# Who copies a finished block out of PSUM, and when two DMAs are issued: two attentions on one core

## The chip, the cores and the metric

The kernel runs on one core of a Trainium2 chip. The metric is the device time of one execution in microseconds. Before the change three runs took 1610.16, 1611.54 and 1611.78 us (median 1611.54).

## The reference

Two attentions over 2048 positions with 576 columns, 32 heads of 18 each, side by side in the output. A is local: each position attends to itself and seven earlier ones at distances of 2, 4, ... 14. B is full softmax attention.

```python
H = 32; Dh = D // H            # D = 576, S = 2048
qkv = (x @ wqkv).reshape(B, S, 3, H, Dh)
# A: idx = pos[:, None] - arange(8) * 2, masked where negative
logits = einsum("bhsd,bhswd->bhsw", q, k[:, :, idx]) * scale
a = einsum("bhsw,bhswd->bhsd", softmax(logits), v[:, :, idx]) @ A_wo
# B: every query with every key
p = softmax(einsum("bhqd,bhkd->bhqk", q, k) * scale)
b = einsum("bhqk,bhkd->bhqd", p, v) @ B_wo
return concatenate([a, b], axis=-1)
```

## The kernel before, in words

All matmuls of projections, scores and output products work on split numbers: a value is held as a rounded high part and a low part (`hi`, `lo`), and a product is the sum of three.

**Stage 1** (the first 410 us or so) makes q, k and v of both attentions and stores them in DRAM (`dqk`, `dv`, `da`).

**Stage 2** is a loop over 512 steps (line 1226). B's 32 heads are 8 groups `g` of four, its queries 4 blocks `b` of 512, its keys 16 tiles `kt` of 128: a step is one `(g, b, kt)`, so a block is 16 steps. In a step

- `score` (L298) makes for each of four heads a product of 128 keys with 512 queries (L305, TensorE) in one of four PSUM banks ("scores"), and ScalarE takes the exponential into `e` (L309);
- three, seldom four, products for later blocks are made in three other banks ("else", L175) and reduced on VectorE to maxima `mx` over keys (L191, L193, L205);
- `weigh` (L769) multiplies the `e` of the step before with v into the bank `po` (L772), which collects a block's 16 steps: for each head 18 sums and the denominator.

The order of the scores and maxima inside a step is written out as a string (L1230 to L1237).

`finish` (L777) follows the last `weigh` of a block: `o` is a copy of `po` in SBUF (L781), and TensorE's next `weigh` needs `po` free. Fixed numbers of steps later (`later`) the denominators go through DRAM (`den`, `drec`, `rec`, L804 to L807), GpSimd multiplies `o` by the reciprocals and splits it (L808 to L810), and it is stored (`do`, L800). Blocks of the last group take a shorter way (`shortly`, `closing`).

The maxima of a block end in the queries' operand `qs`: as rows 54 and 55 they are subtracted inside the score product. `least` (L211) reduces them, `turn` transposes them, `halve` (L225) splits them on GpSimd, `order` (L229) stores them in DRAM (`dm`, L232), and `place` (L235) loads them back into `qs` (L238). Between these stand fixed numbers of steps; from `order` to `place` it is one step in the last group and three elsewhere. A block's first score needs them.

A's local attention is computed in stage 2 by GpSimd, VectorE and ScalarE (`local`, L886) for 8 stretches of 256 positions, 55 steps apart. Its results go to DRAM (`dao`, L980), and `get` (L983) fetches them for 128 positions at a time into the single buffers `at0`, `at1` and `ahl` (L990, L992). Two steps later on, `one` and `two`, hold the output product, one half of the columns each (`sums_of_a`, L1000): 27 matmuls in two banks (L1104), a copy of one sum by ScalarE (L1008), and an add of the other by VectorE (L1009), which is issued behind the step's scores (`behind_scores`, L1251). The steps that hold a product are in the set `producing` (L1040, and L1196 for those of B in the last group); many of them are first steps of a block, in which `finish` runs for the block before.

Every engine works through its instructions in the order in which the program gives them. SP issues nearly all DMAs, and one that has to wait holds all behind it.

Of the kernel before, what the change touches and what calls it, by code (L numbers as in the profile page):

```python
# [10 lines left out]
AF = mybir.ActivationFunctionType  # L11
# [11 lines left out]
NG = H // 4  # L23
# [46 lines left out]
def two_attentions(ctx: ExitStack, tc, xa, wa, woa, xb, wb, wob, out):  # L70
# [5 lines left out]
    nc = tc.nc  # L76
# [29 lines left out]
    po = p_po.tile([128, 512], F32, name="po")  # L106
# [10 lines left out]
    step = 0  # L117

    def later(n, f):
        agenda[step + n].append(f)  # L120
# [44 lines left out]
    def block(g, b):  # L165

        qs, ks = sets[g % 3]
        mx = maxes.tile([128, 2, 2, 4, 6], F32, name="mx", bufs=3)
        left = 2 * 8 * 6
        rest = [[(k, t, p) for k in range(NB) for t in range(4) for p in range(2)] for _ in range(2)]  # L170

        def take(ps, r, k, t, p, at, n):

            rows_ = slice(64 * r, 64 * r + 54)
            return nc.tensor.matmul(ps, qs[rows_, b, p, 128 * t : 128 * t + 128],  # L175
                                    ks[rows_, p, 512 * k + at : 512 * k + at + n], start=True, stop=True)

        def made(n):
            nonlocal left
            left -= n  # L180
            if left == 0:
                later(int(projecting), least)

        def whole(r):
            k, t, p = rest[r].pop(0)
            ps = bank()
            take(ps, r, k, t, p, 0, 512)

            def reduce():
                if k < 2:  # L190
                    nc.vector.tensor_reduce(mx[:, r, p, t, k : k + 1], ps, axis=AX.X, op=ALU.max)  # L191
                else:
                    nc.vector.tensor_reduce(mx[:, r, p, t, 2 * k - 2 : 2 * k], ps.rearrange("q (h n) -> q h n", h=2),  # L193
                                            axis=AX.X, op=ALU.max)
                made(1 + (k > 1))

            return reduce

        def part(i, k, t, p, r, ps, before=None):
            if before:  # L200
                behind_of(nc.tensor.nop(nofuse=True), before)
            ins = take(ps[:, 256 * r : 256 * r + 256], r, k, t, p, 256 * i, 256)

            def reduce():
                nc.vector.tensor_reduce(mx[:, :, p, t, 2 * k - 2 + i], ps.rearrange("q (h n) -> q h n", h=2),  # L205
                                        axis=AX.X, op=ALU.max)
                made(2)

            return ins, reduce

        def least():  # L211
            m = least_rooms[n_least[0] % 2]
            n_least[0] += 1
            nc.vector.tensor_reduce(m[:, :16], mx.rearrange("q r p t k -> q (r p t) k"), axis=AX.X, op=ALU.max,
                                    negate=True)
            later(1, lambda: turn(m))

        def turn(m):

            parts = maxes.tile([128, 2, 32], F32R, name="mt", bufs=2)  # L220
            raw = parts[:, 1].bitcast(F32)
            nc.vector.transpose(raw, m)  # L222
            later(1, lambda: halve(parts, raw))

        def halve(parts, raw):  # L225
            split_on(nc.gpsimd, parts[:, 0], parts[:, 1], raw)
            later(2, lambda: order(parts))

        def order(parts):  # L229

            for k in range(2):
                load(rows(dm[g, b, k, 0, 0], (32, 4), (128, 32), (1, 32)), parts[:, k].bitcast(F32))  # L232
            later(1 if g == NG - 1 else 3, place)

        def place():  # L235
            placed.add((g, b))
            for k in range(2):
                load(qs.bitcast(F32)[54 + k : 128 : 64, b].rearrange("r p n -> r (p n)"),  # L238
                     dm[g, b, k, :16].rearrange("(r i) n -> r (i n)", r=2))

        return rest, whole, part
# [169 lines left out]
    with (tc.tile_pool(name="x", bufs=1, side="right") as xp,  # L411
# [103 lines left out]
        if True:  # L515
# [34 lines left out]
            for c in range(5):  # L550
                one, other = (load, nc.scalar.dma_start) if c % 2 == 0 else (nc.scalar.dma_start, load)
# [159 lines left out]
            for k in range(2, 14):  # L711
                n = 46 if k == 2 else 36 + 4 * k
# [13 lines left out]
            order = [t for i in (0, 8) for j in range(4) for t in (i + j, i + j + 4)]  # L726
# [18 lines left out]
            order = [(c, b) for b0 in range(0, NB, 2) for c in range(2) for b in (b0, b0 + 1)]  # L745
            order += [(c, b) for c in range(2, 14) for b in range(NB)]
            for c, b in order:
                n = min(128, 3 * D - 128 * c)
                work_list.append(((b % 2, ws[c][0], xas[b][0], slice(0, n), every),
                                  lambda ps, n=n: ps[:n], lambda ps, c=c, b=b, n=n: leave_a(c, b, n, ps)))  # L750
# [12 lines left out]
        step = 0  # L763
# [13 lines left out]
    def finish(g, b):  # L777
        o = work.tile([128, 512], F32, name="o", bufs=2)
        if g == NG - 1 and b == NB - 1:
            return closing(b, o, work.tile([128, 512], F32, name="rec", bufs=1))  # L780
        nc.scalar.activation(o, po, AF.Copy)  # L781
        den = work.tile([128, 16], F32, name="den", bufs=2)
        rec = work.tile([128, 512], F32, name="rec", bufs=1)
        parts = []

        def room():
            if g == NG - 1 and b == 0:

                parts[:] = [ap(work.tile([128, 4, 128], F32R, name=f"at{i}", bufs=1), (1, 512)) for i in range(2)]
            else:  # L790
                n = work.tile([128, 2, 512], F32R, name="n", bufs=1)
                parts[:] = n[:, 0], n[:, 1], n
            return parts

        if g == NG - 1 and b > 0:
            return shortly(b, o, rec, *room()[:2])

        def store():
            if g < NG - 1:
                load(do[:, g, :, 512 * b : 512 * b + 512].rearrange("i p n -> p i n"), parts[2].bitcast(F32))  # L800
            else:
                plan(step, full(b, parts))

        for at, f in ((1, lambda: load(den, o[DH:128:32])),  # L804
                      (8, lambda: nc.vector.reciprocal(den, den)),
                      (9, lambda: load(drec[g, b].rearrange("i (p n) -> (i p) n", n=16), den)),
                      (13, lambda: load(rec, rows(drec[g, b], (512, 4), (0, 32), (1, 512)))),  # L807
                      (18, lambda: nc.gpsimd.tensor_mul(o, o, rec)),  # L808
                      (19, lambda: nc.gpsimd.tensor_copy(room()[0], o)),
                      (20, lambda: nc.gpsimd.tensor_sub(parts[1], o, parts[0])),  # L810
                      (26, store)):
            later(at, f)
# [49 lines left out]
    producing = set()  # L862
# [23 lines left out]
    def local(j):  # L886
# [96 lines left out]
        def get(n):  # L983
            st["x"] = []
            st["n"] = n
            last = work.tile([128, 128], F32R, name="ahl", bufs=1)
            for i in range(2):
                t = work.tile([128, 4, 128], F32R, name=f"at{i}", bufs=1)
                for s in range(2):
                    load(t.bitcast(F32)[:, :, SUB * s : SUB * s + SUB],  # L990
                         dao[j, i, 2 * n + s, :512].rearrange("(c p) n -> p c n", p=128))
                load(last.bitcast(F32)[64 * i : 64 * i + 64].rearrange("p (s n) -> p s n", s=2),  # L992
                     rows(dao[j, i, 2 * n, 512], (SUB, 64), (D * SUB, 2), (1, SUB)))
                st["x"].append([t[:, c] for c in range(4)])
            st["x"].append(last)
# [21 lines left out]
        pieces = [(LOWER, lower), (SHARE, share), (UP, upper), (REST, rest), (PUT0, lambda: put(0)), (PUT1, lambda: put(1))]  # L1017
# [12 lines left out]
        start = A_FROM + GAP * j  # L1030
        for n in range(2):
            free, begin = turns[-1] if turns else 0, start + PUT1 + 5
            at = max(free, begin)
            one = next(t for t in TURNS if t >= at + 7)
            two = next(t for t in TURNS if t > one + 1)
            turns.extend((one, two))
            pieces.append((max(at, one - 9) - start, lambda n=n: get(n)))
            for h, t in enumerate((one, two)):
                pieces.append((t - 1 - start, lambda h=h: finished(h)))
                producing.add(t)  # L1040
            pieces.append((two + 5 - start, lambda n=n: load(out[p0 + 128 * n : p0 + 128 * n + 128, :D], ys["a", j, n])))
# [184 lines left out]
    while step < ALL:  # L1226
        n, kt = divmod(step, NT)
        g, b = divmod(n, NB)
        many = min(4 if behind() > 0 else 3, total - int(sum(given)))
        if not inside and many in (1, 3):  # L1230
            order = PLAIN if many > 1 else PLAIN.replace("A", "").replace("B", "")
        else:
            places = positions(many)
            order = "".join("%d%s" % (h, "BA"[h % 2] if h in places else "") for h in range(4))
            if inside:
                at = order.index("3" if 3 in places else "2") if step % NT != AT or AT == 0 else FIRST
                order = order[:at] + "+" + order[at:]  # L1237
# [56 lines left out]
```

## Time and profile before

| | us |
|---|---|
| median of three runs | 1611.54 |
| profiled execution | 1610.11 |
| its span, first to last instruction | 1608.3 |
| TensorE (PE) busy | 1597.4 |
| VectorE (DVE) busy | 1388.4 |
| ScalarE (ACT) busy | 1213.3 |
| GpSimd (POOL) busy | 962.0 |
| exponentials L309, 2048 of 608 ns | 1047.2 |
| maxima L191, L193, L205, 2048 of 682 to 685 ns | 1365.7 |

Busy time counts an instruction from start to end. Instructions of one engine overlap (the exponentials start about 0.51 us apart), so a sum of durations can be more than the time that they take. The profile shows the whole execution from the first to the last instruction of the core; the device time is 1.8 us longer. PEld is TensorE's loading of weights ahead of a matmul. In a timeline row stand start and duration in us, engine, line, operation, output and input, shapes and count, and in brackets the idle time of the engine before it with what ended it. SPq is SyncE's queue of DMA issues.

### The profile page before, as it was taken

How to read it: one execution, taken by the hardware profiler on the slowest of the kernel's cores; microseconds unless marked ns; L12 is line 12 of the kernel's file. 1: busy time of each engine (PE TensorE's matmuls, PEld its weight loads, DVE VectorE, ACT ScalarE, POOL GpSimd, SP SyncE). 2: the span in 40 equal slices, each digit the busy share in tenths (PEclk: the TensorE clock that was granted, in tenths of full speed). 3: DMA queues.
4: the chain of work that ended last, by engine and by line, in shares of the span. 5: the costliest groups of instructions: out<-in, count | busy, mean ns of one | idle time of the engine just before them, and what ended most of it. 6: DMA issues, size and time to landing. Idle time of an engine off the chain costs nothing.

```text
span 1608.3 us, 34964 instructions
## 1 busy us (share of the span) xinstructions
PE 1597.4 (99%) x13360; PEld 956.0 (59%) x13360; DVE 1388.4 (86%) x2350; ACT 1213.3 (75%) x2421; POOL 962.0 (60%) x816
## 2 busy tenths in 40 slices
PE   9999999999999999999999999999999999999998
PEld 7999999999544444444444444444444444444776
DVE  5199999999999999999999999999999999998533
ACT  6323432121699999999999999999999999997454
POOL 2305742210256997985995994995994996930100
PEclk9999999999999999999999999999999999999999
DMA  8937954532322353164136135323523232234211
GB/s 256 232 125 206 258 181 123 143 105 80 61 58 56 72 114 103 38 132 117 46 90 162 43 83 151 80 63 99 134 60 93 58 85 76 80 122 138 84 39 60
DMA packets 190150, 173.13 MB, mean 108 GB/s; under 512 B 123120, under 2 KB 136944, under 8 KB 188256
## 3 DMA queue, kind: packets, MB, share of 16 engines
q1 hardware_dynamic: 185120, 159.36, 35.8%
q0 software_dynamic: 4032, 10.63, 3.2%
q8 instruction: 106, 1.74, 0.5%
q10 hardware_dynamic: 832, 0.92, 0.2%
q14 instruction: 60, 0.49, 0.1%
HBM read 97.47 MB, written 72.95 MB: 106 GB/s over the span
## 4 chain that ended last, share of the span: by engine, by line
PE 98%; DVE 1%; DMA 0%; SPq 0%; ACT 0%; issue 0%; POOL 0%; ACTq 0%; POOLq 0%; DVEq 0%
PE po L772 31%; PE bank L305 19%; PE bank L175 19%; PE bank L394 17%; PE bank L1104 7%; PE bank L331 5%; DVE mx L191 0%; PE bank L546 0%; DMA qs<-dm 0%; DMA out<-y 0%; DVE mx L193 0%; PE bank L1079 0%; ACT vs L612 0%; DVE rec L843 0%; POOL xlo L442 0%
## 5 line engine op out<-in xcount | busy, mean ns | idle before, releaser
L309 ACT ACTIVATE e<-bank 128x512 f32<-128x512 f32 x2048 | 1047.2, 608 | 58.8 <-PE bank L305 51.8
L175 PE MATMUL bank<-ks,qs 54*128 54x512 f32 (+1 forms) x2502 | 784.0, 381 | 1.0 <-DVE mx L191 0.5
L191 DVE TENSOR_REDUCE mx<-bank 128x1 f32<-128x512 f32 x1024 | 682.6, 685 | 87.7 <-PE bank L175 65.1
L175 PEld LDWEIGHTS bank<-ks,qs 54*128 54x128 f32 x2502 | 398.2, 184 | 431.5 <-DVE mx L205 348.2
L305 PE MATMUL bank<-qs,ks 56*128 56x512 f32 x2048 | 574.5, 426 | 3.4 <-DMA qs<-dm 3.4
L772 PE MATMUL po<-e,v 128*19 128x512 f32 x4096 | 538.3, 600 | 0.0
L193 DVE TENSOR_REDUCE mx<-bank 128x2 f32<-128x512 f32 x570 | 373.4, 685 | 32.8 <-PE bank L175 21.5
L305 PEld LDWEIGHTS bank<-qs,ks 56*128 56x128 f32 x2048 | 302.5, 185 | 45.0 <-ACT e L309 34.4
L205 DVE TENSOR_REDUCE mx<-bank 128x2 f32<-128x512 f32 x454 | 309.7, 682 | 0.0
L962 POOL TENSOR_TENSOR pr<-lg,akv 128x1024 f32<-128x1024 f32 x72 | 157.2, 2205 | 0.6
L772 PEld LDWEIGHTS po<-e,v 128*19 128x19 f32 x4096 | 70.6, 97 | 132.2 <-issue 123.6
L722 ACT ACTIVATE ohi<-bank 128x512 f32<-128x512 f32 (+1 forms) x56 | 30.4, 595 | 154.5 <-issue 101.5
L394 PE MATMUL bank<-xhi,ahi 64*128 64x512 f32 (+1 forms) x448 | 120.2, 390 | 0.0
L394 PE MATMUL bank<-xhi,alo 64*128 64x512 f32 (+1 forms) x448 | 114.1, 390 | 0.0
L394 PE MATMUL bank<-xlo,ahi 64*128 64x512 f32 (+1 forms) x448 | 109.3, 391 | 0.1
L914 POOL TENSOR_TENSOR pr<-aq,akv 128x1024 f32<-128x1024 f32 x40 | 87.9, 2204 | 10.7 <-PE bank L175 9.6
L964 POOL TENSOR_TENSOR pr<-pr 128x512 f32<-128x512 f32 x72 | 91.4, 1292 | 0.6
L442 POOL TENSOR_TENSOR alo<-raw,ahi 128x512 fp32r<-128x512 f32 (+1 forms) x14 | 17.6, 1258 | 111.9 <-ACT ahi L441 100.1
L534 POOL TENSOR_TENSOR olo<-olo,ohi 128x512 fp32r<-128x512 f32 x36 | 46.2, 1297 | 61.9 <-ACT ohi L533 57.3
L917 POOL TENSOR_TENSOR pr<-pr,aohi 128x1024 f32<-128x1024 f32 x32 | 76.6, 2393 | 0.6
L917 POOL TENSOR_TENSOR pr<-pr 128x1024 f32<-128x1024 f32 x32 | 76.4, 2388 | 0.0
L112 POOL CAST mt<-mt 128x32 fp32r<-128x32 f32 x32 | 6.8, 213 | 111.1 <-DVE mt L222 111.1
(200 smaller groups left out, 2093.1 us busy)
## 6 DMA issues: line engine op xcount, KB each, us to landing
do<-n SPq DMA_DIRECT2D x28, 512.0 KB
da<-ohi SPq DMA_DIRECT2D x52, 256.0 KB
akv<-da SPq DMA_DIRECT2D x64, 175.5 KB
out<-y SPq DMA_DIRECT2D x32, 288.0 KB
qs<-dqk SPq DMA_DIRECT2D x30, 288.0 KB
ks<-dqk SPq DMA_DIRECT2D x30, 288.0 KB
at<-dao SPq DMA_DIRECT2D x64, 128.0 KB
rec<-drec SPq DMA_DIRECT2D x29, 256.0 KB
```

The costliest lines, as they stand in the source:

```text
L175: return nc.tensor.matmul(ps, qs[rows_, b, p, 128 * t : 128 * t + 128], ks[rows_, p, 512 * k + at : 512 * k + at + n], start=True, stop=True)
L191: nc.vector.tensor_reduce(mx[:, r, p, t, k : k + 1], ps, axis=AX.X, op=ALU.max)
L193: nc.vector.tensor_reduce(mx[:, r, p, t, 2 * k - 2 : 2 * k], ps.rearrange("q (h n) -> q h n", h=2), axis=AX.X, op=ALU.max)
L205: nc.vector.tensor_reduce(mx[:, :, p, t, 2 * k - 2 + i], ps.rearrange("q (h n) -> q h n", h=2), axis=AX.X, op=ALU.max)
L305: nc.tensor.matmul(ps, ks[at, p, 128 * kt : 128 * kt + 128], qs[at, b, p], start=True, stop=True)
L309: nc.scalar.activation(e, ps, AF.Exp, scale=SCALE)
L394: nc.tensor.matmul(ps, a, b, start=start, stop=stop)
L772: nc.tensor.matmul(po[32 * i : 32 * i + 19], vs[g][:, kt, 19 * i : 19 * i + 19], es[i], start=kt == 0, stop=kt == NT - 1)
L917: nc.gpsimd.tensor_add(st["prs"][0], st["prs"][0], st["prs"][c - 1])
L962: nc.gpsimd.tensor_mul(at, ap(st["lg"], (0, 2), (SUB, W), (1, SUB)), window(st["v"], n))
L964: nc.gpsimd.tensor_add(at[:, :, :4], at[:, :, :4], at[:, :, 4:])
L1104: nc.tensor.matmul(ps, a, b, start=start, stop=stop)
```

## The change

Three edits. `order` is called one step after `halve` in the last group, two steps after it in the others as before. `finish` copies `po` with VectorE where the running step is in `producing`, with ScalarE elsewhere. A fetch of local results that was due in the step `at` (the step in which its buffers' last product runs, or five steps after the results' store) is due at `at + 1` at the earliest.

```diff
         def halve(parts, raw):
             split_on(nc.gpsimd, parts[:, 0], parts[:, 1], raw)
-            later(2, lambda: order(parts))
+            later(1 if g == NG - 1 else 2, lambda: order(parts))
...
         o = work.tile([128, 512], F32, name="o", bufs=2)
         if g == NG - 1 and b == NB - 1:
             return closing(b, o, work.tile([128, 512], F32, name="rec", bufs=1))
-        nc.scalar.activation(o, po, AF.Copy)
+        if step in producing:
+            nc.vector.tensor_copy(o, po)
+        else:
+            nc.scalar.activation(o, po, AF.Copy)
...
-            pieces.append((max(at, one - 9) - start, lambda n=n: get(n)))
+            pieces.append((max(at + 1, one - 9) - start, lambda n=n: get(n)))
```

## The prediction, made before the changed kernel ran

> **What bounds the kernel now.** I read the page first (span, busy time, chain), then the waits of TensorE, then the timeline at each place where its steps are longer than usual.
>
> ```profile
> span 1608.3 us, 34964 instructions
> ...
> PE 1597.4 (99%) x13360; PEld 956.0 (59%) x13360; DVE 1388.4 (86%) x2350; ACT 1213.3 (75%) x2421; POOL 962.0 (60%) x816
> ...
> PE 98%; DVE 1%; DMA 0%; SPq 0%; ACT 0%; issue 0%; POOL 0%; ACTq 0%; POOLq 0%; DVEq 0%
> ```
>
> TensorE is busy for all but 11 us, and the chain that ended last is 98% TensorE. Its waits as the trace lists them have one large entry, and it is on the path:
>
> ```profile
> PE bank L305 <- DMA qs<-dm: 3.4, 1, 3.4
> ```
>
> That is one score matmul waiting for the maxima of its block to come back from DRAM. The timeline there (start, duration, engine and line; the L772 rows are the `po` group that ends every step):
>
> ```profile
> 1468.25 1.05 PE L772 MATMUL po<-e,v 128*19 128x512 f32 x8
> ...
> 1469.23 0.38 PE L175 MATMUL bank<-ks,qs 54*128 54x256 f32 x1
> 1472.98 0.47 PE L305 MATMUL bank<-qs,ks 56*128 56x512 f32 x1 [3.36 <-DMA qs<-dm]
> ...
> 1473.96 1.90 PE L772 MATMUL po<-e,v 128*19 128x512 f32 x8
> ...
> 1477.54 1.05 PE L772 MATMUL po<-e,v 128*19 128x512 f32 x8
> ```
>
> Two steps took 1477.54 - 1468.25 = 9.29 us. The step after the wait is slow too: its `po` group takes 1.90 us where others take 1.05. The granted clock in the stretches behind the wait (columns: stretch, length, busy time and count of PE, PEld, DVE, ACT, POOL, then PEclk) says why:
>
> ```profile
> 1474.00:1475.80 1.80, 1.80 (x11) 0.12 (x10) 1.40 (x3) 1.54 (x4) 0.10 (x1) 0.51 0.45 162
> 1475.80:1477.50 1.70, 1.70 (x12) 1.33 (x8) 0.67 (x2) 1.48 (x3) 0.00 (x0) 0.52 0.46 169
> ```
>
> For 3.5 us TensorE ran at half its clock, so the 3.4 us wait cost more than itself.
>
> **Maxima a step sooner, fetch a step later (edits 1 and 3).** Who was late? SP's own timeline has the store of these maxima, a fetch of local results, and the load that the score waits for; the chain has the load's flight:
>
> ```profile
> 1453.60 1.23 SPq L232 DMA_DIRECT2D dm<-mt  x2
> 1463.79 0.93 SPq L990 DMA_DIRECT2D at<-dao  x2
> ...
> 1467.98 1.06 SPq L238 DMA_DIRECT2D qs<-dm  x2
> ```
> ```profile
> 1468.56 4.28 DMA qs<-dm
> ```
>
> The maxima were stored by 1454.8, but SP stood at the fetch until 1463.79, because its tiles were still read by the output product of the running step; the load behind it was issued only at 1467.98. In the changed program's order of instructions the two `qs<-dm` and the `rec<-drec` stand ahead of this fetch, behind the same store. Where nothing stands between store and load, the gap is the store's flight:
>
> ```profile
> 1370.71 1.18 SPq L232 DMA_DIRECT2D dm<-mt  x2
> 1371.94 0.47 SPq L1041 DMA_DIRECT2D out<-y  x1
> 1372.74 1.12 SPq L238 DMA_DIRECT2D qs<-dm  x2
> ```
>
> So 2.0 us from store to load: the load would be issued at about 1453.6 + 2.0 = 1455.6, its second half by 1456.7, and with the 4.28 us of flight it lies in SBUF by 1461, 8 us before 1469.2. The fetch waits for the same product, so it isn't issued before 1463.8, nor later: with a `rec` load of about 0.6 SP is through by 1457.4. The other SP moves are swaps of two or three neighbours (an output store or a `drec` store behind the maxima); five of the 16 fetches of local results go one step later and still have six or more steps (six of 2.04 us are 12 us) to their product, against the 4.28 us of flight above. I cost all of these at nothing; what covers them is that slack, and TensorE's waits name no other DMA.
>
> What a step with a block's end costs without such a wait, when ScalarE copies `po` and no product is in it:
>
> ```profile
> 1004.30 1.05 PE L772 MATMUL po<-e,v 128*19 128x512 f32 x8
> ...
> 1006.38 1.05 PE L772 MATMUL po<-e,v 128*19 128x512 f32 x8
> ...
> 1008.78 1.05 PE L772 MATMUL po<-e,v 128*19 128x512 f32 x8
> ```
>
> 2.08 + 2.40 = 4.48 us for the two steps. The place at 1468 is of that kind (480 isn't a product step, so its copy stays on ScalarE). Saved: 9.29 - 4.48 = **4.8 us**. Bounds: 3.4 if only the listed wait goes, 5.2 if both steps went at 2.04.
>
> [...]
>
> **The copy on VectorE (edit 2).** The orders of instructions of the two programs differ by 22 copies gone from ScalarE and 22 put on VectorE, each right behind the add of the product's halves (L1009). One is in the last stretch, where VectorE idles between products (46.9 us ahead of L1123, a row below); I cost it at nothing. The other 21 look nearly alike. One of them:
>
> ```profile
> 1145.83 0.50 PE L305 MATMUL bank<-qs,ks 56*128 56x512 f32 x1
> ...
> 1146.02 0.60 ACT L781 ACTIVATE o<-po 128x512 f32<-128x512 f32 x1 [0.51 <-issue]
> ...
> 1146.48 0.69 DVE L191 TENSOR_REDUCE mx<-bank 128x1 f32<-128x512 f32 x1 [0.48 <-PE bank L175]
> 1146.51 6.69 ACT L309 ACTIVATE e<-bank 128x512 f32<-128x512 f32 x13
> ...
> 1146.88 1.05 PE L772 MATMUL po<-e,v 128*19 128x512 f32 x8
> 1147.09 0.68 DVE L205 TENSOR_REDUCE mx<-bank 128x2 f32<-128x512 f32 x1
> 1147.69 1.52 DVE L191 TENSOR_REDUCE mx<-bank 128x1 f32<-128x512 f32 x2
> ...
> 1148.62 0.18 PEld L305 LDWEIGHTS bank<-qs,ks 56*128 56x128 f32 x1
> ...
> 1149.05 1.05 PE L772 MATMUL po<-e,v 128*19 128x512 f32 x8
> ...
> 1151.09 1.05 PE L772 MATMUL po<-e,v 128*19 128x512 f32 x8
> ...
> 1152.69 0.18 PEld L175 LDWEIGHTS bank<-ks,qs 54*128 54x128 f32 x1
> ```
>
> What is there to win: the steps here are 2.17 (1146.88 to 1149.05) and 2.04 us (to 1151.09). So the block's end costs 0.14 us, not 0.4 as without a product: ScalarE has been waiting in the product step (0.51 idle). The 0.14 comes from the fourth score, loaded at 1148.62, whose bank the fourth exponential of the step before must leave. ScalarE starts that row of exponentials at 1146.51, behind the copy; without it, it would start when the first score (1145.83 + 0.50) is there, at about 1146.35: 0.16 sooner, enough for the 0.14.
>
> What it costs: no row has a VectorE copy of this shape. The nearest:
>
> ```profile
> L191 DVE TENSOR_REDUCE mx<-bank 128x1 f32<-128x512 f32 x1024 | 682.6, 685 | 87.7 <-PE bank L175 65.1
> ...
> L1123 DVE COPY y<-bank 128x288 f32<-128x288 f32 x24 | 10.9, 455 | 46.9 <-PE bank L1104 46.9
> ```
>
> 0.455 us for 288 columns is below it, 0.685 for a reduce of the same 512 columns from PSUM beside it; I take 0.69, with the next one starting 0.60 behind (as 1147.09 follows 1146.48). `po` is complete at the time that ScalarE's copy shows, 1146.02; VectorE stands idle then (0.48 before 1146.48). It copies to 1146.71, before TensorE wants `po` at 1146.88. The first reduce moves from 1146.48 to 1146.62, 0.14 late, and those behind it with it. Does TensorE feel that? The third reduce, at 1147.69, would end at 1147.83 + 0.69 = 1148.52. Its bank is wanted 1.60 behind the `po` group before (1152.69 - 1151.09 in the undisturbed step), so at 1148.48. Late by 0.14, less the 0.10 that there was to spare (1148.48 against 1147.69 + 0.69), costs about 0.05. Net per end: -0.14 + 0.05 = -0.09, and VectorE, with three starts of 0.60 in a 2.04 us step, has made the rest good one step later. Bounds: -0.14 (nothing felt) to +0.46 (all 0.60 felt).
>
> [...]
>
> Four ends differ. At 1110.62 ScalarE has an exponential of the local part behind the copy:
>
> ```profile
> 1111.11 0.62 ACT L941 ACTIVATE lg<-lg 128x512 f32<-128x512 f32 x1
> ...
> 1111.47 1.05 PE L772 MATMUL po<-e,v 128*19 128x512 f32 x8
> ...
> 1114.17 1.05 PE L772 MATMUL po<-e,v 128*19 128x512 f32 x8
> ```
>
> That step is 2.70, 0.66 too long; with the copy gone this exponential fits into ScalarE's idle time: -0.6. At three ends VectorE has small work in the gap. The worst:
>
> ```profile
> 1360.17 0.34 DVE L952 RECIPROCAL as<-as 128x32 f32<-128x32 f32 x1
> ...
> 1360.43 0.20 DVE L214 TENSOR_REDUCE m<-mx 128x16 f32<-128x96 f32 x1
> ...
> 1360.72 0.69 DVE L191 TENSOR_REDUCE mx<-bank 128x1 f32<-128x512 f32 x1
> ```
>
> There the first reduce moves by the copy's whole 0.60, which costs 0.5 behind the spare 0.10, less 0.1 won: +0.4. The two others (a maximum of the local part at 863, a transpose at 688, each smaller) I put at +0.2 and 0. Sum: 17 x -0.09 - 0.6 + 0.6 = **-1.5 us**; bounds -3.4 (all of 20 x 0.14 and 0.6 won) to +1.0 (the 0.14 given back everywhere and the three full).
>
> **Sum.** 1610.11 (the profiled execution: span 1608.3 and 1.8 around it) - 4.8 - 1.5 = 1603.8. The three runs lie at 1610.16, 1611.54 and 1611.78; from their median the same sum gives 1605.2. I take the middle, 1604.6.
>
> **Rivals.**
> *The copy stalls the maxima (slower).* Mechanism: VectorE runs three reduces of 0.60 in a step of 2.04, and if the copy waits for `po` in VectorE's order while banks are needed, each end costs up to its full 0.60, so 21 x 0.46 = +9.7, less 4.8: 1611.54 + 4.9 = 1616. From 0.23 us felt per end more than won (4.8 / 21) the kernel is slower. Against it: the 0.48 us of idle time ahead of the first reduce, and 2.04 - 3 x 0.60 = 0.24 us of slack in each step. Chance 0.07.
> *The change does not reach the wait.* Another thing holds the load or the fetch (SP stops at `rec<-drec`, the fetched results then come late for step 484), and the wait only moves: the copies alone, 1611.54 - 1.5 = 1610. For it: SP is one queue. Against: the store is out by 1454.8 and 14 us are left. Chance 0.08.
> *The clock part isn't there in most runs.* Without it the slow groups take back 0.85 + 0.7 = 1.55 us, and only 3.3 are saved: 1611.54 - 3.3 - 1.5 = 1606.8. Against it: the timed runs are longer than the profiled one, which has the slow clock. Chance 0.10.
> *Forecast:* wait and slow clock gone, copies between -3.4 and +1.0: 1602 to 1607.5, chance 0.75.
>
> **Numbers.** The range 1602.0 to 1608.9 leaves out the two first rivals and a little at the lower end. A measurement can tell about 0.2%, 3.2 us, from no change. Faster by more than that (below 1608.3): forecast and clock rival, 0.85. Within: most of the second rival, 0.08. Slower: 0.07.
>
> **What would show it.** No wait of TensorE for `qs<-dm`, PEclk 1.0 through 1469 to 1478, `po` groups 2.08 and 2.40 apart there; SP issuing `qs<-dm` about 2 us behind the store, before the fetch. At the 21 ends a VectorE copy of 0.66 to 0.70 us, the second step behind the product at 2.04 to 2.10 instead of 2.17, the one that ended at 1114 near 2.1, the one behind 1361 longer by 0.4. I am wrong if these steps stay at 2.17 or above, if a new wait for `at<-dao` or `rec<-drec` shows on TensorE, or if the last 130 us (from 1478 on) get longer.

## The result and the profile after

The changed kernel takes 1604.72 us (median of five runs, 1604.08 to 1606.24) against 1611.47 us (1610.03 to 1611.78) for the kernel before: a ratio of 0.9962, 95% interval 0.9951 to 0.9972. That is 6.7 us. The profiled execution took 1604.72 us, with a span 5.4 us shorter than before's.

The page after, span and busy times:

```profile
span 1602.9 us, 34949 instructions
...
PE 1595.1 (100%) x13360; PEld 944.4 (59%) x13360; DVE 1400.5 (87%) x2372; ACT 1203.0 (75%) x2399; POOL 961.6 (60%) x816
```

VectorE has 12 us more and ScalarE 10 us less: the 22 copies. TensorE's waits no longer name a DMA; the longest is one at the start of the kernel, which was there before:

```profile
PE bank L546 <- DVE raw L544: 1.5, 1, 1.5
```

**At the place of the wait.** SP's timeline in the changed kernel (line numbers behind L781 are three higher):

```profile
1442.41 6.70 SPq L1070 DMA_DIRECT2D ks<-do  x8
...
1452.84 1.23 SPq L232 DMA_DIRECT2D dm<-mt  x2
1460.71 1.14 SPq L238 DMA_DIRECT2D qs<-dm  x2
1461.94 0.55 SPq L810 DMA_DIRECT2D rec<-drec  x1
1463.05 0.92 SPq L993 DMA_DIRECT2D at<-dao  x2
```

The load stands ahead of the fetch now and is issued 7 us sooner than before (1467.98). But it is not issued 2 us behind the store: the gap is 7.9 us. The `po` groups there, and the granted clock (the third column from the right) over the whole place:

```profile
1467.50 1.05 PE L772 MATMUL po<-e,v 128*19 128x512 f32 x8
...
1469.54 1.05 PE L772 MATMUL po<-e,v 128*19 128x512 f32 x8
...
1471.63 1.05 PE L772 MATMUL po<-e,v 128*19 128x512 f32 x8
...
1474.02 1.05 PE L772 MATMUL po<-e,v 128*19 128x512 f32 x8
```
```profile
1460.00:1480.00 20.00, 19.78 (x175) 10.52 (x172) 18.66 (x33) 16.87 (x34) 1.28 (x1) 1.00 0.49 132
```

The place has to be read over three steps. ScalarE's copy of the block that ends here starts at 1475.95 in the kernel before and at 1470.95 in the changed one, so the group that ends the block is the one at 1473.96 there and at 1469.54 here. The kernel before has one group more, behind those of the prediction:

```profile
1479.56 1.05 PE L772 MATMUL po<-e,v 128*19 128x512 f32 x8
```

From 1468.25 to 1479.56 it took 11.31 us (5.71 + 3.58 + 2.02); the changed kernel takes 2.04 + 2.09 + 2.39 = 6.52 (1467.50 to 1474.02), at full clock. That is 4.79 less.

**At an end of a block in a product step.** The same end as in the prediction (some rows left out):

```profile
1145.28 0.69 DVE L782 COPY o<-po 128x512 f32<-128x512 f32 x1
...
1145.62 6.79 ACT L309 ACTIVATE e<-bank 128x512 f32<-128x512 f32 x13 [0.87 <-PE bank L305]
...
1145.89 0.68 DVE L191 TENSOR_REDUCE mx<-bank 128x1 f32<-128x512 f32 x1
...
1146.12 1.05 PE L772 MATMUL po<-e,v 128*19 128x512 f32 x8
...
1147.09 1.38 DVE L191 TENSOR_REDUCE mx<-bank 128x1 f32<-128x512 f32 x2
...
1147.73 0.18 PEld L305 LDWEIGHTS bank<-qs,ks 56*128 56x128 f32 x1
...
1147.82 0.18 PEld L175 LDWEIGHTS bank<-ks,qs 54*128 54x128 f32 x1
...
1148.24 1.05 PE L772 MATMUL po<-e,v 128*19 128x512 f32 x8
```

The second step is 2.12 (1146.12 to 1148.24), where it was 2.17. ScalarE starts its exponentials 0.34 behind the time at which `po` is complete, instead of 0.49. VectorE's third reduce ends at 1147.09 + 0.68 = 1147.77, and TensorE loads the weights for its bank at 1147.82: now this is the last one that the step waits for.

**The worst end**, near 1359 us:

```profile
1359.20 0.69 DVE L782 COPY o<-po 128x512 f32<-128x512 f32 x1
...
1359.81 0.34 DVE L955 RECIPROCAL as<-as 128x32 f32<-128x32 f32 x1
1360.04 1.05 PE L772 MATMUL po<-e,v 128*19 128x512 f32 x8
1360.07 0.19 DVE L214 TENSOR_REDUCE m<-mx 128x16 f32<-128x96 f32 x1
1360.18 0.67 DVE L191 TENSOR_REDUCE mx<-bank 128x1 f32<-128x512 f32 x1
...
1362.53 1.05 PE L772 MATMUL po<-e,v 128*19 128x512 f32 x8
```

The copy pushes two small operations and the first reduce back; the step takes 2.49 where it took 2.13.

Where the time went is read from the starts of the `po` groups in both traces. Behind the end at 452 the changed kernel's run is 0.18 us later than before's (it was as late at the first group, so stage 1 took that much longer), behind the end at 1432 it is 0.76 earlier: 0.94 gained. Behind the place of the wait it is 5.56 earlier: 4.80 there. The last group is 5.66 earlier, but the 12.5 us behind it take 0.3 longer, which leaves the 5.4 of the span; what lengthens them was not followed. The 0.94 is rough: over the same stretch the second profile of the kernel before is 0.33 slower than the first. The steps at the 21 ends themselves are the better measure: they add up to 1.0 us less in the changed kernel, to 1.1 less in the other profiles with the same copies, and to the same within 0.05 in those with ScalarE's copies.

### The profile page after: what moved, and what is told of

Its sections match the earlier page's. It is cut to its first block, busy times and chain, and to the rows that moved or that the text cites. A ratio compares the mean times of both kernels' runs of the same rounds, so it can differ in the third digit from the quotient of the medians.

```text
span 1602.9 us, 34949 instructions
## 1 busy us (share of the span) xinstructions
PE 1595.1 (100%) x13360; PEld 944.4 (59%) x13360; DVE 1400.5 (87%) x2372; ACT 1203.0 (75%) x2399; POOL 961.6 (60%) x816
## 4 chain that ended last, share of the span: by engine, by line
PE 98%; DVE 1%; ACT 0%; DMA 0%; issue 0%; POOL 0%; ACTq 0%; POOLq 0%; DVEq 0%
PE po L772 31%; PE bank L305 19%; PE bank L175 19%; PE bank L394 17%; PE bank L1107 8%; PE bank L331 5%; PE bank L546 0%; DVE mx L191 0%; DMA out<-y 0%; DVE mx L193 0%; PE bank L1082 0%; ACT vs L612 0%; DVE rec L846 0%; POOL xlo L442 0%; DVE wlo L442 0%
```

## The experiments

Times are medians; the kernel before ran beside each on the same chip. My theory going in: the wait and the clock behind it are worth 4.8 us, the copies about 1. The main rival: it is the copies that count.

**Copies alone** (both DMA edits undone).

```diff
-        nc.scalar.activation(o, po, AF.Copy)
+        if step in producing:
+            nc.vector.tensor_copy(o, po)
+        else:
+            nc.scalar.activation(o, po, AF.Copy)
```

> Only the copy edit; the maxima of the last group and the fetches as before. My theory: the wait for qs<-dm of about 3.4 us stays on TensorE near 1468 us, with slow po groups (1.9 us) and a granted clock near 0.5 behind it; the 21 ends with a product gain as in the changed kernel (second step 2.12 instead of 2.18, the one near 1111 gains 0.65, those near 864 and 1360 lose 0.1 and 0.4): 0.8 to 1.2 us faster than before, so about 1610.3. Rival (the copies bring most of the gain, the DMA edits little): 4 us or more faster. [...]

Measured: 1610.91 against 1610.99 us, ratio 0.9999 (0.9989 to 1.0008): no gain to be measured, where I expected about 1. Yet the copies do win in this trace: from the end at 452 to that at 1432 it gains 0.96 us on the kernel before. It loses 1.2 at the wait (TensorE's timeline, then the clock):

```profile
1467.63 1.05 PE L772 MATMUL po<-e,v 128*19 128x512 f32 x8
...
1472.63 0.76 PE L305 MATMUL bank<-qs,ks 56*128 56x512 f32 x1 [3.64 <-DMA qs<-dm]
...
1474.39 1.91 PE L772 MATMUL po<-e,v 128*19 128x512 f32 x8
1478.02 1.14 PE L772 MATMUL po<-e,v 128*19 128x512 f32 x8
```
```profile
1471.00:1479.00 8.00, 6.37 (x31) 2.89 (x31) 3.62 (x6) 4.60 (x9) 1.27 (x1) 0.57 0.45 162
```

The two steps take 10.39 us instead of 9.29. The wait is a little longer (3.64), and the first matmul behind it is slow already: 0.57 of full clock over 8 us is (1 - 0.57) x 8 / 0.5 = 6.9 us at half clock.

**DMA edits alone** (the copies back on ScalarE).

```diff
-        if step in producing:
-            nc.vector.tensor_copy(o, po)
-        else:
-            nc.scalar.activation(o, po, AF.Copy)
+        nc.scalar.activation(o, po, AF.Copy)
```

> Both DMA edits, the copies back on ScalarE. My theory: no wait for qs<-dm, granted clock 1.0 throughout, the two steps near 1468 take 4.48 instead of 9.29 us, every end with a product again 2.18 in its second step: 4.8 us faster than before, so about 1606.6. Rival (the DMA edits bring little): within 1.5 us of before.

Measured: 1605.45 against 1610.99 us, ratio 0.9967 (0.9955 to 0.9980), 5.5 us faster. In its trace the place of the wait gives 4.81 us, and every end with a product takes what it took in the kernel before again, most of them 2.17 to 2.19. The rival that the copies bring most of the gain has fallen.

**Each DMA edit by itself.** First the maxima a step sooner:

```diff
-            later(2, lambda: order(parts))
+            later(1 if g == NG - 1 else 2, lambda: order(parts))
```

> Only the maxima of the last group a step sooner. In the program's order the load qs<-dm then stands ahead of the fetch of local results. My theory: this alone takes the wait away, span about 4.8 us shorter (1603.5). Rival (both DMA edits are needed, since the store is late as well as the load): a wait for qs<-dm of 1 us or more stays.

Then the fetch a step later:

```diff
-            pieces.append((max(at, one - 9) - start, lambda n=n: get(n)))
+            pieces.append((max(at + 1, one - 9) - start, lambda n=n: get(n)))
```

> Only the fetch of local results a step later. The load qs<-dm then stands behind rec<-drec, but ahead of the fetch. My theory: what held the load was the fetch ahead of it, so this alone takes the wait away too, span about 4.8 us shorter (1603.5), with the same store-to-load gap as in the changed kernel (near 8 us). Rival (the step of the store decides): the wait of 3.4 us stays.

Measured: single executions of 1606.24 and 1605.40 us, spans 1604.5 and 1603.6, and neither has a wait of TensorE for `qs<-dm`. In both SP issues the load ahead of the fetch, 6.6 us behind the store. So either edit alone takes the wait away. They are not quite alike: by the `po` groups the later fetch gives the whole 4.80 at this place, the sooner maxima 4.38. With the maxima alone `rec<-drec` still stands behind the fetch (1467.75), GpSimd's product with it starts at 1473.65 (1464.60 with the later fetch alone), and VectorE stands for that before it goes on to the maxima:

```profile
1474.96 0.45 DVE L824 STREAM_TRANSPOSE rec<-o 128x256 f32<-128x256 f32 x1 [0.74 <-POOL o L808]
```

The step there takes 2.47 us, where it takes 2.03 with both edits. Each is one profile.

**Three ends back on ScalarE.**

```diff
-        if step in producing:
+        if step in producing and step not in (128, 208, 432):
```

> The changed kernel with the copy back on ScalarE at the three ends (steps 128, 208, 432) where VectorE has small work between the copy and the first reduce. My theory: these three give back what they lost in the changed kernel (0.05, 0.12 and 0.4 us), the 18 others keep their gain: span 0.6 us shorter than the changed kernel's (1602.3), time 1604.1. In its second step the end near 1359 takes 2.13 again instead of 2.49. Rival (the long step near 1359 comes from the local part itself and not from the copy ahead of it): it stays at 2.4 or more on either engine.

Measured: 1603.88 against 1610.86 us, ratio 0.9955 (0.9940 to 0.9970); span 1601.8. At the worst end:

```profile
1357.49 1.05 PE L772 MATMUL po<-e,v 128*19 128x512 f32 x8
1359.52 1.05 PE L772 MATMUL po<-e,v 128*19 128x512 f32 x8
1361.65 1.05 PE L772 MATMUL po<-e,v 128*19 128x512 f32 x8
```

2.03 and 2.13 again. It was the copy ahead of the small work, not the small work. From 452 to 1432 this kernel gains 1.46 on before, where the changed kernel gains 0.94: the three ends cost 0.5.

**All ends on VectorE.**

```diff
-        if step in producing:
-            nc.vector.tensor_copy(o, po)
-        else:
-            nc.scalar.activation(o, po, AF.Copy)
+        nc.vector.tensor_copy(o, po)
```

> The changed kernel with VectorE copying at every end of a block, those without a product too (8 of the first 29, and the one near 1471). My theory: without a product VectorE has only 0.16 us of idle time ahead of its first reduce, so the copy makes it 0.3 to 0.4 late, which costs 0.2 to 0.3 beyond the spare 0.10, about what ScalarE's copy cost there (0.06 + 0.36): these ends stay within 0.15 us of 4.48 for their two steps, those with more VectorE work in the gap (519, 552, 618) get 0.2 to 0.3 longer; in all within 0.8 us of the changed kernel. Rival (VectorE always has room for a copy, ScalarE never): 0.4 us saved at each of 9 ends, 3.5 us faster than the changed kernel.

Measured: 1605.25 us, ratio 0.9961 (0.9947 to 0.9976): like the changed kernel (1604.7 and 1604.8 in its two sets of runs), as I expected, and 4 us away from the rival. The first end, without a product:

```profile
452.01 1.05 PE L772 MATMUL po<-e,v 128*19 128x512 f32 x8
...
453.40 0.68 DVE L781 COPY o<-po 128x512 f32<-128x512 f32 x1
454.00 0.68 DVE L193 TENSOR_REDUCE mx<-bank 128x2 f32<-128x512 f32 x1
454.14 1.05 PE L772 MATMUL po<-e,v 128*19 128x512 f32 x8
...
456.36 1.05 PE L772 MATMUL po<-e,v 128*19 128x512 f32 x8
```

Five ends like this one take 4.35 to 4.37 (here 2.13 + 2.22), 0.13 less than with ScalarE. Those at 519, 552 and 618, with small work behind the copy, take 4.56, 4.52 and 4.70 where they took 4.48, and the last also slows the step behind it by 0.06. The ninth, at the place of the wait, wins 0.12 in its two steps and loses more in the next two (2.12 for 2.03, 4.90 for 4.75), where transposes of `o` (L824) stand between VectorE's maxima. The signs are right; a clean end gains more than the nothing that I had reckoned.

**The copy made twice.**

```diff
-            nc.vector.tensor_copy(o, po)
+            for _ in range(2 if step < STEPS * (NG - 1) + 32 else 1):
+                nc.vector.tensor_copy(o, po)
```

> The changed kernel with the copy of po made twice on VectorE at the 21 ends with a product (the second writes the same values). This takes the cover away: the second copy ends at about 1.3 us behind the start of the first, 0.45 after TensorE wants po, and the first reduce starts 0.74 late. My theory: every 0.60 more on VectorE is then felt nearly in full, 0.55 to 0.65 us at each of 21 ends: 12 to 13 us slower than the changed kernel, about 1617, slower than the kernel before. Rival (VectorE's slack of 0.24 us a step takes it up over the next steps): 3 us or less.

Measured: 1620.33 us, ratio 1.0055 (1.0040 to 1.0070): 15.6 us slower than the changed kernel, more than I expected. One end:

```profile
1189.02 1.05 PE L772 MATMUL po<-e,v 128*19 128x512 f32 x8
...
1190.21 1.42 DVE L783 COPY o<-po 128x512 f32<-128x512 f32 x2 [0.23 <-POOL o L812]
...
1191.54 0.68 DVE L191 TENSOR_REDUCE mx<-bank 128x1 f32<-128x512 f32 x1
1191.68 1.05 PE L772 MATMUL po<-e,v 128*19 128x512 f32 x8 [0.56 <-DVE o L783]
...
1193.90 1.05 PE L772 MATMUL po<-e,v 128*19 128x512 f32 x8
```

TensorE stands for `po` (0.56), that step is 2.66 instead of 2.03, and the next is 2.22 instead of 2.13: 0.73 us for one more copy of 0.69. So nothing beyond the first copy is covered. It is not quite the slower rival of the prediction: 0.63 of the 0.73 is TensorE standing for `po` itself, which the second copy still reads, and only the 0.10 in the next step comes from maxima that are late. What late maxima cost, the worst end shows (0.36).

**The older results loaded later.**

```diff
-            plan(STEPS * g, [(4, lambda: fetch_old(0)), (24, lambda: fetch_old(1)), ...
+            plan(STEPS * g, [(4, lambda: fetch_old(0)), (31, lambda: fetch_old(1)), ...
```

> The changed kernel with the eight loads of 252 KB of older results (ks<-do), issued ahead of the last group's third store of maxima, moved seven steps later, behind the load of the maxima and the fetch. My theory: the 7.9 us from that store to the load (where I had reckoned 2.0) are those loads still in flight on the DMA engines; with them gone it falls to 2 to 3 us, the load is issued near 1455, and nothing else changes in time (within 1 us of the changed kernel's span), since TensorE wants the maxima only at 1469. Rival (the store itself is slow there, or SP's wait is for something else): the gap stays at 6 us or more.

Measured: one execution of 1605.18 us, span 1603.4. SP's timeline:

```profile
1453.27 1.22 SPq L232 DMA_DIRECT2D dm<-mt  x2
1455.34 1.53 SPq L238 DMA_DIRECT2D qs<-dm  x2
...
1467.04 6.19 SPq L1070 DMA_DIRECT2D ks<-do  x8
```

Store to load is 2.1 us. The 7.9 us in the changed kernel were the eight loads (2 MB) that SP had issued just ahead.

**Kernels once more, and the best places.** The kernel before and the copies alone got a second profile, the changed kernel a second set of runs, and a version put together from the two experiments on places ran beside it:

```diff
-        if step in producing:
+        if step not in (48, 64, 96, 128, 208, 432, 480):
             nc.vector.tensor_copy(o, po)
```

> Both DMA edits, and VectorE copies at every end but seven: the six at which small VectorE work stands between the copy and the first reduce (steps 48, 64, 96, 128, 208, 432) and step 480. Put together from the two experiments before: the 18 good ends with a product keep their gain, the three bad ones take 2.18 or 2.13 again, and five ends without a product take 4.35 instead of 4.49 for their two steps (0.13 each). My theory: 0.6 + 0.7 = 1.2 to 1.3 us faster than the changed kernel on the same chip, about 1603.4, span 1601.5. Rival (the gains don't add up, because what ScalarE is spared at one end VectorE lacks at the next): within 0.4 us of the changed kernel.

> The changed kernel again, to stand beside the one above on the same chip. Expected: about 1604.8, no wait for qs<-dm, the ends as in its first profile within 0.02 us a step, the store-to-load gap of the third maxima again between 6 and 8 us.

> The kernel before again, for a second profile of its wait. My theory: the wait for qs<-dm is again 3.3 to 3.7 us, and a stretch of granted clock near 0.5 follows it, but it need not start and end at the same distance from the wait (it was 3.5 us long in the first profile of this kernel, some 5 us in that of the copies alone). If the clock follows the wait alone, stretch and price are those of the first profile: slow from 1 us behind the wait's end, 3.5 us long, two steps of 9.3 us in all.

> The copies alone again (both DMA edits undone), for a second profile. In the first the copies had won about 1.0 us by 1432 us, and the place of the wait took 1.2 us more than in the kernel before, by a longer stretch of slow clock. If that was chance, the place now takes between 8.9 and 10 us for its two steps, the same spread as the kernel before; if the copies lengthen the wait, it is again 10 us or more while the kernel before stays at 9.3.

Measured, same chip, kernel before at 1611.13 us: best places 1603.04 us (1602.86 to 1603.36), ratio 0.9952 (0.9938 to 0.9965); changed kernel 1604.83 us (1604.44 to 1605.79), ratio 0.9963 (0.9950 to 0.9975). The version with chosen places is 1.8 us faster than the changed kernel by the medians; by the `po` groups from 452 on it is 1.3 to 1.5 faster, as put together. It beats both kernels. The changed kernel's store-to-load gap was 7.2 us this time.

The kernel before: one execution of 1611.17 us, with the wait and the clock as in its first profile:

```profile
1474.02 0.47 PE L305 MATMUL bank<-qs,ks 56*128 56x512 f32 x1 [3.44 <-DMA qs<-dm]
...
1475.01 1.88 PE L772 MATMUL po<-e,v 128*19 128x512 f32 x8
...
1478.59 1.05 PE L772 MATMUL po<-e,v 128*19 128x512 f32 x8
```

The copies alone: 1611.71 us, the longer price again:

```profile
1472.98 0.76 PE L305 MATMUL bank<-qs,ks 56*128 56x512 f32 x1 [4.41 <-DMA qs<-dm]
...
1474.74 1.91 PE L772 MATMUL po<-e,v 128*19 128x512 f32 x8
1478.37 1.50 PE L772 MATMUL po<-e,v 128*19 128x512 f32 x8
```

Its two steps take 11.2 us (from 1467.20), after a gain of 1.06 by 1432. Both profiles of this kernel show it, so chance alone is less likely than I had put it; with ten runs showing no gain either, the copies alone seem to lose at the wait what they win before. The mean granted clock on record for each timed run leans the same way: 0.997 in six of the ten and 0.998 in four, against 0.998 or 0.999 in all 15 of the kernel before beside them. It is no sharp line, since two of nine runs of the kernel before on the second chip have 0.997 too. Why the wait is longer there is only in part seen: SP's issue of `rec<-drec`, ahead of the load, took 0.88 and 0.98 us instead of 0.57, and the load's flight 4.3 and 4.9 us. What lengthened these stays open.

## Why the prediction was right, point by point

1. **The bound.** TensorE, by one wait and by its steps: shown. The experiments that moved the time did so through these two.
2. **The wait is the fetch's doing.** Shown by either DMA edit alone: the load ahead of the fetch, no wait. The rival that the change does not reach the wait has fallen. **4.8 us** was the forecast for this term; the trace gives 4.80 in the changed kernel and 4.81 with the DMA edits alone (5.5 by the medians). The working has a slip that happened to cost nothing: it set the 9.29 us against the 4.48 of an undisturbed end, but those two steps lie one step further on, from the block's last group (1473.96 in the kernel before). The 9.29 become 4.13; the 2.39 of the end falls into the next step, which took only 2.02 in the kernel before: ScalarE's copy was done there within the slow step of 3.58. An ordinary step is 2.04, so the wrong pair gave the right difference.
3. **The load near 1455, 8 us ahead of need.** Wrong, without consequence. I took the 2.0 us from a place where nothing large was in flight (the mean DMA share was 0.00 from 1366 to 1370). Here eight loads were (a share of 0.46 to 0.51 from 1453 to 1459), and the gap was 7.9 us (2.1 with them moved). With a flight like that of before (4.28 us, from the second half's issue at 1461.35) the maxima were there some 3 us ahead of their score (1468.49) instead of 8: an estimate, the landing is in no view; the step that failed is "the gap is the store's flight".
4. **The clock.** Part of the 4.8 us is the half clock behind the wait (0.50 for 3.4 us). That it might be missing in most runs was a rival: it was there in all four profiles with the wait. What I had not seen is that its length comes in two sizes, 3.4 and 6.8 us (below).
5. **The copy's price.** 0.69 forecast, 0.690 to 0.693 measured, with the next operation 0.61 behind its start (1145.28 to 1145.89; forecast 0.60).
6. **A plain end: -0.09 forecast, -0.05 to -0.07 measured at 16 of the 17, -0.12 at the one near 652.** ScalarE is earlier as reckoned; the spare of VectorE's third reduce was smaller. I took 0.10 between its end and the load of the next weights as free, but 0.05 of that is needed when the load does wait (1147.77 to 1147.82). So the 17 give -1.0 instead of -1.5: this is the mis-sized term.
7. **The odd ends.** Near 1111: 2.05 after 2.70, -0.65 (forecast -0.6). Near 1359: +0.36, and 0.05 in the step behind it (forecast +0.4). The other two +0.05 and +0.11 (forecast 0 and +0.2).
8. **Sum.** Forecast 4.8 + 1.5; the trace shows 4.8 + 0.94, less 0.2 that the runs differ by at the start and 0.2 behind the place of the wait: 5.4. The middle between profile and median, put at 1604.6 (its figures give 1604.5), met the 1604.72; part of that is luck: the copies gave 0.5 less than forecast, while the step from median to median (6.7) is larger than that between the profiled executions (5.4), because the profiled execution of the kernel before was one of its fastest. One sign of being wrong was a longer stretch behind 1478: it is 0.2 longer. The profiles scatter as much there (the copies alone 0.4 longer, the DMA edits alone 0.1 shorter than the kernel before), so this neither speaks against the mechanism nor is it explained.
9. **The slower rival.** 0.46 per end was to be its price. The worst end paid about 0.4 of it, with small work in VectorE's gap; put back on ScalarE, the three such ends gave 0.5 back. The copy made twice costs 0.73 for each further copy, mostly by another way (`po` is held), and is slower than the kernel before. Both show that the cover that I named, VectorE's idle time behind the product, is what the change lives on.

## What to carry to other kernels

SP's queue handed its wait at the fetch to everything behind it (the load went out at 1467.98 behind the fetch, at 1460.71 ahead of it): a small load that the critical engine needs belongs ahead of a fetch that waits for that engine itself, and here moving either past the other was enough (4.80 and 4.38 us at that place). A copy moved between two busy engines paid at the ends where the receiving engine had room at that very moment (0.05 to 0.12 us at each plain end), and cost where small work already stood there (0.36 us at the worst end); chosen place by place it was worth more than by one rule for all places (1.8 us by the medians). And a saving ahead of a wait can vanish in it, as it seems to have done with the copies alone (0.96 and 1.06 us won by 1432, no gain in the medians), so remove the wait first and then measure.

## What the runs showed of the hardware

**The half clock behind the wait lasted 3.4 or 6.8 us.** In each row stand a stretch, its length, how long TensorE was busy in it and with how many instructions, then the granted clock, the DMA share and GB/s. The kernel before (the stretch ahead of the half clock, and the half clock itself), then the copies alone, second profile (the half clock):

```profile
1470.62:1474.03 3.41, 1.05 (x11) 1.00 0.43 147
1474.03:1477.44 3.41, 3.41 (x16) 0.50 0.45 165
```
```profile
1472.51:1475.92 3.41, 2.94 (x15) 0.50 0.42 150
1475.92:1479.34 3.42, 3.42 (x20) 0.50 0.45 166
```

In the kernel before the half clock lasts 3.4 us in both profiles and starts 1.05 and 1.08 us after TensorE had gone back to work. In the copies alone it lasts 6.8 us in both (by the 0.57 above, 6.9) and starts inside the wait (at 1472.51 in the second profile, where TensorE goes back to work at 1472.98). So the lengths are once and twice 3.4 us. The 3.4 us ahead of the half clock in the kernel before (1470.62 to 1474.03), still at a granted clock of 1.00, hold 2.4 us of idle time, up to 1472.98.

Cut into stretches of 3.41 us, counted from where the half clock begins, the four profiles agree on more. The stretch ahead of the half clock was busy for 1.05 and 1.08 us in the kernel before, 0.97 and 0.00 in the copies alone; the one before that was busy for 2.30 to 3.42 us, and the granted clock behind it was still 1.00. The half clock ended with the first stretch that was busy throughout. In the kernel before that was the first at half clock; in the copies alone the first was busy for only 2.21 and 2.94 us, and a second followed. That the busy time of the first stretch decides between one and two of them is a reading of these four profiles, not tried by itself; what sets the 3.4 us, no run shows.

**A small store behind large loads.** The 32 KB of maxima took 6.6 to 7.9 us until SP could issue the load that reads them, in the profiles in which this load stands ahead of the fetch and 2 MB of loads were issued just before on the same queue (7.9 and 7.2 in the changed kernel), and 2.1 us in the one without those loads.
